# The PSUM banks of an MLP as tiles of their own, in a pool opened behind the first batch's attention

## The chip, the cores and the metric

The kernel runs on one core of a Trainium2 chip. The core has five engines with instruction queues of their own: TensorE (PE, the matmuls; PEld is its loading of weights), VectorE (DVE), ScalarE (ACT), GpSimd (POOL) and SyncE (SP), which here only issues DMA transfers. Matmuls write to PSUM, a memory of eight banks of 2 KB in each of 128 partitions; VectorE and ScalarE carry results from there to SBUF ("evacuate" them). The metric is the device time of one execution in microseconds (us); lower is better.

## What is computed

Four batches of causal-window attention with eight heads (sequence 768, head dimension 64), and then a Fourier mix with a two-layer MLP over its output:

```
scores = q @ k.T / 8 + bias                    # kept: 96 local keys, 8 global keys
a = exp(scores - max) / sum
x = (a @ v), heads side by side                # (4, 768, 512)
u = x + real(fft over the sequence and over the 512 columns)
un = (u - mean(u)) / sqrt(var(u) + 1e-6)
out = u + max(un @ w_ch1, 0) @ w_ch2           # w_ch1: 512 x 2048, w_ch2: 2048 x 512
```

## The kernel before

The work of a batch goes through these steps. `trans` turns q and k of two heads (L392, transposes on TensorE into a PSUM tile `pt`); `score` multiplies them (L420, into `sc`), ScalarE takes the exponential (`er`, L439), VectorE multiplies by the mask (`ex`, L449); `v_global` and `glob` treat the eight global keys; `av` multiplies with v (L519, L532, into `pav`) and VectorE divides (`rc` L549, `x` L550). The Fourier mix follows: folds on VectorE (`eA`, `ww`, `zy`, L592 to L661), matmuls `py` (L683, L686), mirrored copies on GpSimd, matmuls `pu` (L763), the sum `u` (L780), statistics (L789, L791) and `rstd` on GpSimd, the normalised `un` (L809, L811) and its transposes `ptu` (L827) into `unT` (L835, L837).

The MLP then runs in 12 groups `c` of 256 rows, three to a batch. The first layer is `ph_unit(c, jp)`, eight units to a group: eight matmuls of 128x256 (L855) into one bank `ph`, and one evacuation with the ReLU into `hT`, on ScalarE (L861) or VectorE (L862). The second layer is `pg_unit(c, t, part)`: for each of the two output tiles `t`, four parts of four matmuls of 128x512 (L878) that add up in one bank `pg`; then VectorE adds `u` (`ob`, L889) and SyncE stores it (L893).

The order of all instructions is fixed while the program is written: a planner (`Plan`) keeps an estimated time for each engine and picks from four streams (Fourier mix, attention, first layer, second layer) the step that can start first by its own table of costs. For the MLP it counts two free banks for `ph` and two for `pg` (`RING`). It also decides which of ScalarE and VectorE evacuates. Each engine then works through its instructions in order; the framework under the kernel puts in the waits, from which tiles an instruction reads and writes.

PSUM is split as follows. The tag `xx` has two tiles of two banks, used by all of attention and the Fourier mix. The other four banks are two tiles `c0` and `c1` of two banks each, allocated once and never given back (`cd`). While the first batch's attention runs, they are two more places for its scores and products (tags `C` and `D`). After that, a unit of the first layer writes one half of `c0`, in turn, and an output tile of the second layer one half of `c1`:

```
if tag in turn:
    turn[tag] += 1
    return cd["ph pg".index(tag) // 3][:, turn[tag] % 2, :]
```

A unit of the first layer may not be planned before all 22 uses of `C` and `D` in the first batch are through (the token `("CD",)`).

Of the kernel before, what the change touches and what calls it, by code (L numbers as in the profile page):

```python
# [10 lines left out]
FP32 = mybir.dt.float32  # L11
# [3 lines left out]
P = 128  # L15
# [156 lines left out]
def kernel(  # L172
# [69 lines left out]
    ps = ctx.enter_context(tc.tile_pool(name="ps", bufs=1, space=bass.MemoryType.PSUM))  # L242
# [3 lines left out]
    RING = {"xx": 2, "ph": 2, "pg": 2}  # L246
    pl.rings = {r: [0.0] * n for r, n in RING.items()}

    cd = [ps.tile([P, 2, 512], FP32, tag=f"c{i}", name=f"c{i}", bufs=1) for i in range(2)]
    pl.rings["C"] = [0.0]  # L250
    pl.rings["D"] = [0.0]
    turn = {"ph": 0, "pg": 0}

    def bank(tag, name, dtype=FP32):

        if tag in "CD":
            return cd["CD".index(tag)]
        if tag in turn:
            turn[tag] += 1
            return cd["ph pg".index(tag) // 3][:, turn[tag] % 2, :]  # L260
        return ps.tile([P, 2, 512 if dtype == FP32 else 1024], dtype, tag=tag, name=name, bufs=RING[tag])


    NBUF = {"hT": 3, "vs": 2, "qk": 2, "qs": 3, "qkT": 4, "er": 2, "eg": 1, "x": 1, "xr": 1, "zy": 1, "eA": 1,
# [118 lines left out]
    def trans(b, hp):  # L383
        n = HP * b + hp

        def run(start, ring):
            pt = bank("xx", f"pt_{n}", FP16)
            src = qk16.pop(n)
            for w in range(2):
                for j in range(NS):  # L390
                    o = pt[:, w, (j // 2) * 256:(j // 2) * 256 + 256].rearrange("p (a t m) -> p t a m", a=2, t=2)
                    nc.tensor.transpose(o[:, j % 2], src[:, w, j].rearrange("p h d -> p (h d)"), idn)  # L392
            e = pl.pe(mm_us(P, 2 * NS), start)
            pl.used(("free", "qk", n), e)

            def evac():
                TT[n] = buf("qkT", n, [P, 2, S], FP16, 6)
                V.tensor_copy(TT[n], pt[:, :, 0:S])  # L398
            pl.later([("DVE", dve2(2 * S), evac)], free("qkT", n), e, [("qkT", n)], ring=ring, rank=RA(b))
            for s in range(2):  # L400
                def cp(s=s):
                    c0 = 16 * (hp % 2) + 8 * s
                    nc.gpsimd.tensor_copy(  # L403
                        kG[b % 2][64 * s:64 * s + 64, hp, c0:c0 + NG].rearrange("p (j m) -> p j m", j=2),
                        TT[n][64 * s:64 * s + 64, 1, 0:P].rearrange("p (j m) -> p j m", j=2)[:, :, 0:NG // 2])
                pl.later([("POOL", 0.2, cp)], [("qkT", n)] + ([("gldone", b - 2, hp // 2)] if b > 1 else []), 0.0,
                         [("kG", n, s)], [("free", "qkT", n)], rank=RA(b))
        ATT.append(([("qk", n, 0), ("qk", n, 1)], ("xx",), run))

    def score(b, hp, g):  # L410
        n = HP * b + hp
        idx = 3 * n + g

        def run(start, ring):
            pa = bank(ring, f"sc_{n}_{g}")
            w0, w1_ = ((256, CO), (CO, CO), (256, P))[g]
            for i, c0, cw in ((2 * g, 0, w0), (2 * g + 1, 256, w1_)):
# [37 lines left out]
    def v_global(b, halves):  # L455
        def run(start, ring):
            pv = bank(ring, f"pvg_{b}_{halves[0]}")
            for half in halves:
                for h in range(4):
                    nc.tensor.matmul(pv[32 * half:32 * half + 32, 0, h * 64:(h + 1) * 64],  # L460
                                     sel_sb[:, h * 32:(h + 1) * 32],
                                     v16[b % 2][:, 0, 4 * half + h, 0:Dh], start=True, stop=True,
                                     tile_position=(0, 32 * half))
            e = pl.pe(mm_us(64, 4 * len(halves)), start)
            rows = slice(32 * halves[0], 32 * halves[-1] + 32)
            dst = vG[b % 2][rows, :, 0:Dh]
            src = pv[rows, 0, 0:256].rearrange("p (h d) -> p h d", d=Dh)
            pl.later([("ACT", act(256), lambda: A(dst, src, AF.Copy)),
                      ("DVE", dve(256), lambda: V.tensor_copy(dst, src))],
                     [("avdone", b - 2)] if b > 1 else [], e, [("vG", b, half) for half in halves], CD(b), ring=ring, rank=RA(b))  # L470
        ATT.append(([("v", b, 2 * half + i) for half in halves for i in range(2)] + [("one", 0)], BANKS(b), run))
# [581 lines left out]
```

## Time and profile before

| | us |
|---|---|
| median of 3 runs | 342.33 |
| lowest and highest | 341.27 to 342.86 |
| the profiled execution | 341.82 |
| its span, first to last instruction | 340.1 |
| TensorE busy | 269.9 |
| VectorE busy | 192.7 |
| ScalarE busy | 117.0 |
| GpSimd busy | 82.8 |

The span is the stretch that the profile shows; the execution's time holds 1.7 us more around it. Busy times count an engine's instructions as the profiler records them; matmuls are pipelined, and the record of the last one before a pause is longer than the time until the next one could have been issued. "c" in the rows stands for `c0` and `c1`, since buffer numbers are left out.

In order of time: up to 57 us the first batch's attention and its Fourier mix, with the loads of the weights; then three times a stage in which the first layer is mixed with the next batch's attention (from 57, 139 and 214 us) and one with that batch's Fourier mix and the second layer (from 106, 181 and 253 us); from 283 us the MLP alone, for what is left of it.

### The profile page before, as it was taken

How to read it: one execution, taken by the hardware profiler on the slowest of the kernel's cores; microseconds unless marked ns; L12 is line 12 of the kernel's file. 1: busy time of each engine (PE TensorE's matmuls, PEld its weight loads, DVE VectorE, ACT ScalarE, POOL GpSimd, SP SyncE). 2: the span in 40 equal slices, each digit the busy share in tenths (PEclk: the TensorE clock that was granted, in tenths of full speed). 3: DMA queues.
4: the chain of work that ended last, by engine and by line, in shares of the span. 5: the costliest groups of instructions: out<-in, count | busy, mean ns of one | idle time of the engine just before them, and what ended most of it. 6: DMA issues, size and time to landing. Idle time of an engine off the chain costs nothing.

```text
span 340.1 us, 5796 instructions
## 1 busy us (share of the span) xinstructions
PE 269.9 (79%) x2360; PEld 179.8 (53%) x2360; DVE 192.7 (57%) x348; ACT 117.0 (34%) x165; POOL 82.8 (24%) x165
## 2 busy tenths in 40 slices
PE   0687266888899796687889799977798998888984
PEld 0454154766665354566566356665574565666531
DVE  2579956553468968455368859655458487100011
ACT  7384022435640023345632132544621113323300
POOL 1351058335533505503005123300000053000000
PEclk9997565899999999599999999999999999999999
DMA  9999899999896950300205411000024301000011
GB/s 191 225 234 223 156 233 206 226 216 219 169 223 162 271 189 34 92 2 16 78 2 139 138 49 61 33 3 0 3 48 109 123 34 62 2 31 2 31 62 62
DMA packets 66091, 37.04 MB, mean 109 GB/s; under 512 B 26641, under 2 KB 61713, under 8 KB 66065
## 3 DMA queue, kind: packets, MB, share of 16 engines
q1 hardware_dynamic: 61840, 32.48, 39.9%
q0 software_dynamic: 4224, 4.19, 7.5%
q8 instruction: 18, 0.29, 0.4%
q14 instruction: 9, 0.07, 0.1%
HBM read 31.42 MB, written 9.44 MB: 120 GB/s over the span
## 4 chain that ended last, share of the span: by engine, by line
PE 59%; DVE 17%; ACT 10%; SPq 5%; issue 3%; POOL 3%; DMA 2%; DVEq 0%; POOLq 0%; ACTq 0%
PE c L855 27%; PE c L878 19%; ACT hT L861 8%; DVE hT L862 5%; DVE ob L889 3%; PE pav L532 3%; SPq L339 2%; DMA u<-in_v_dram 2%; PE py L683 2%; SPq L314 2%; PE pu L763 2%; PE py L686 1%; DVE x L550 1%; PE pav L519 1%; PE sc L420 1%
## 5 line engine op out<-in xcount | busy, mean ns | idle before, releaser
L855 PE MATMUL c<-unT,w 128*128 128x256 f16 x768 | 97.6, 278 | 25.4 <-ACT hT L861 17.4
L878 PE MATMUL c<-w,hT 128*128 128x512 f16 x384 | 91.4, 379 | 10.0 <-DVE ob L889 9.8
L855 PEld LDWEIGHTS <-w 128*128 128x128 f16 x768 | 75.1, 99 | 45.6 <-issue 34.5
L861 ACT ACTIVATE hT<-c 128x512 f16<-128x512 f32 x68 | 38.5, 595 | 86.9 <-PE c L855 68.5
L878 PEld LDWEIGHTS <-hT 128*128 128x128 f16 x384 | 36.7, 98 | 48.9 <-issue 13.9
L862 DVE TENSOR_SCALAR hT<-c 128x512 f16<-128x512 f32 x28 | 19.2, 691 | 49.5 <-PE c L855 48.4
L439 ACT ACTIVATE er<-sc 128x768 f16<-128x768 f32 (+2 forms) x42 | 38.3, 925 | 20.1 <-PE sc L420 9.9
L889 DVE TENSOR_TENSOR ob<-c,u 128x512 f32<-128x512 f32 x24 | 16.5, 689 | 45.9 <-PE c L878 45.9
L354 POOL CAST qk<-qs 128x768 f16<-128x768 f32 x24 | 23.1, 980 | 36.9 <-issue 34.5
L449 DVE TENSOR_TENSOR ex<-er,mk 128x992 f16<-128x992 f16 (+2 forms) x48 | 30.7, 657 | 0.4 <-ACT er L439 0.4
L699 ACT ACTIVATE zy<-py 128x512 f16<-128x512 f32 (+1 forms) x12 | 9.6, 810 | 58.9 <-PE py L686 47.9
L732 POOL COPY ww<-zy 128x512 f16<-128x512 f16 x16 | 9.4, 614 | 64.2 <-PE py L683 46.0
L403 POOL COPY kG<-qkT 64x8 f16<-64x8 f16 x32 | 9.9, 311 | 51.8 <-DVE qkT L398 51.0
L392 PE MATMUL pt<-ident,qk 128*128 128x128 f16 x192 | 16.5, 247 | 3.2 <-DVE qk L352 1.3
L683 PE MATMUL py<-t,ww 128*128 128x256 f16 x48 | 12.4, 308 | 7.8 <-DVE ww L646 6.9
L398 DVE COPY qkT<-pt 128x1536 f16<-128x1536 f16 x16 | 15.2, 952 | 5.5 <-PE pt L392 5.5
L809 ACT ACTIVATE un<-u,rstd 128x512 f16<-128x512 f32 x13 | 10.3, 808 | 22.2 <-POOL rstd L799 22.2
L392 PEld LDWEIGHTS <-qk 128*128 128x128 f16 x192 | 14.4, 112 | 5.7 <-issue 3.0
L420 PE MATMUL sc<-qkT 64*128 64x256 f16 (+2 forms) x168 | 15.2, 273 | 2.7 <-DVE u L780 2.1
L780 DVE TENSOR_TENSOR u<-pu,xr 128x1024 f32<-128x1024 f32 x12 | 14.4, 1219 | 4.6 <-PE pu L763 4.6
L532 PEld LDWEIGHTS <-ex 128*128 128x128 f16 x352 | 13.6, 100 | 5.7 <-issue 1.7
L532 PE MATMUL pav<-v,ex 128*128 128x65 f16 x308 | 15.3, 196 | 0.0
(89 smaller groups left out, 278.0 us busy)
## 6 DMA issues: line engine op xcount, KB each, us to landing
out_dram<-ob SPq DMA_DIRECT2D x24, 256.0 KB, 2.0
qs<-in_q_dram SPq DMA_DIRECT2D x13, 384.0 KB, 6.1
qs<-in_k_dram SPq DMA_DIRECT2D x13, 384.0 KB, 4.5
vs<-in_v_dram SPq DMA_DIRECT2D x24, 192.0 KB, 6.0
w<-in_moe_w_ch_dram POOLq DMA_DIRECT2D x8, 512.0 KB, 11.9
xd<-x SPq DMA_DIRECT2D x16, 192.0 KB, 3.6
xr<-xd SPq DMA_DIRECT2D x8, 384.0 KB, 3.8
u<-in_v_dram SPq DMA_DIRECT2D x8, 192.0 KB, 6.1
```

Of the source, the lines that this page charges most:

```text
L354: nc.gpsimd.tensor_copy(d, s)
L392: nc.tensor.transpose(o[:, j % 2], src[:, w, j].rearrange("p h d -> p (h d)"), idn)
L420: nc.tensor.matmul(pa[:, s, c0:c0 + cw], TT[n][lo:lo + 64, 1, i * P:(i + 1) * P], TT[n][lo:lo + 64, 0, i * P:i * P + cw], start=True, stop ...
L439: A(mine(), cut(pa), AF.Exp, 0.0, 0.125)
L449: VT(o, mine(), m, op=ALU.mult)
L532: nc.tensor.matmul(po[:, jj, hh * 65:(hh + 1) * 65], lhsT, v16[b % 2][:, i, h, 0:65], start=(jp == 0 and a == 0), stop=(a == len(ops) - 1) ...
L683: nc.tensor.matmul(o, wr, t1_sb[:, rs, 128:384], start=True, stop=(wi is None))
L855: nc.tensor.matmul(ph[:, a * CH:(a + 1) * CH], w1[:, d, jb * P:(jb + 1) * P], UNT[c][:, d, :], start=(d == 0), stop=(d == ND - 1))
L861: pl.later([("ACT", act(512), lambda: A(dst, ph, AF.Relu)), ("DVE", dve(512), lambda: V.tensor_scalar_max(dst, ph, 0.0))], [], e, [("h", c ...
L862: ("DVE", dve(512), lambda: V.tensor_scalar_max(dst, ph, 0.0))],
L878: nc.tensor.matmul(pg, HT[c][:, jb, t * P:(t + 1) * P], w2[:, jb, :], start=(jb == 0), stop=(jb == NJ - 1))
L889: VT(cell[0], pg, UT[c][:, t, :], op=ALU.add)
```

## The change

The four banks are no longer two tiles that stay. The early places `C` and `D` come from a pool of their own (`pse`), and each use allocates a tile anew. When the first bank for the MLP is asked for, that pool is closed and another (`psl`) is opened in its place, and from then on each unit of the first layer gets a tile of one bank under the tag `ph`, each output tile one under `pg`, with two buffers to a tag. The planner's numbers are untouched. Lines below the change are two higher than before (L855 becomes L857, L861 becomes L863, L878 becomes L880).

```diff
@@ -246,19 +246,21 @@
     RING = {"xx": 2, "ph": 2, "pg": 2}
     pl.rings = {r: [0.0] * n for r, n in RING.items()}
 
-    cd = [ps.tile([P, 2, 512], FP32, tag=f"c{i}", name=f"c{i}", bufs=1) for i in range(2)]
     pl.rings["C"] = [0.0]
     pl.rings["D"] = [0.0]
-    turn = {"ph": 0, "pg": 0}
+
+    early = {"ctx": tc.tile_pool(name="pse", bufs=1, space=bass.MemoryType.PSUM)}
+    early["pool"] = early["ctx"].__enter__()
 
     def bank(tag, name, dtype=FP32):
-
-        if tag in "CD":
-            return cd["CD".index(tag)]
-        if tag in turn:
-            turn[tag] += 1
-            return cd["ph pg".index(tag) // 3][:, turn[tag] % 2, :]
-        return ps.tile([P, 2, 512 if dtype == FP32 else 1024], dtype, tag=tag, name=name, bufs=RING[tag])
+        if tag in ("C", "D"):
+            return early["pool"].tile([P, 2, 512], FP32, tag=tag, name=name, bufs=1)
+        if tag == "xx":
+            return ps.tile([P, 2, 512 if dtype == FP32 else 1024], dtype, tag=tag, name=name, bufs=RING[tag])
+        if "late" not in early:
+            early["ctx"].__exit__(None, None, None)
+            early["late"] = ctx.enter_context(tc.tile_pool(name="psl", bufs=1, space=bass.MemoryType.PSUM))
+        return early["late"].tile([P, 512], FP32, tag=tag, name=name, bufs=RING[tag])
 
 
     NBUF = {"hT": 3, "vs": 2, "qk": 2, "qs": 3, "qkT": 4, "er": 2, "eg": 1, "x": 1, "xr": 1, "zy": 1, "eA": 1,
```

On every engine the instructions stand in the same order as before. What changes is what they wait for. On ScalarE, in the end phase (the eight units of group 10; `hT` is the ReLU's output, `c_66` is `c0`), before:

```order
L861 ACTIVATE hT_3415<-c_66 128x512
L861 ACTIVATE hT_3415<-c_66 128x512 [waits PE_49]
L861 ACTIVATE hT_3415<-c_66 128x512
L861 ACTIVATE hT_3415<-c_66 128x512 [waits PE_49]
L861 ACTIVATE hT_3415<-c_66 128x512
L861 ACTIVATE hT_3415<-c_66 128x512 [waits PE_49]
L861 ACTIVATE hT_3415<-c_66 128x512
L861 ACTIVATE hT_3415<-c_66 128x512 [waits PE_49]
```

and with the change:

```order
L863 ACTIVATE hT_3531<-ph_0_3532 128x512 [waits PE_49]
L863 ACTIVATE hT_3531<-ph_1_3549 128x512 [waits PE_49]
L863 ACTIVATE hT_3531<-ph_2_3558 128x512 [waits PE_49]
L863 ACTIVATE hT_3531<-ph_3_3573 128x512 [waits PE_49]
L863 ACTIVATE hT_3531<-ph_4_3582 128x512 [waits PE_49]
L863 ACTIVATE hT_3531<-ph_5_3597 128x512 [waits PE_49]
L863 ACTIVATE hT_3531<-ph_6_3608 128x512 [waits PE_49]
L863 ACTIVATE hT_3531<-ph_7_3625 128x512 [waits PE_49]
```

Before, every second evacuation waits for TensorE and the one behind it for nothing; now each one waits for TensorE, and each reads a tile of its own.

On TensorE, at the same place in the program (where the second unit of a pair follows the first, and then where the next pair follows a part of the second layer, whose output `c_67` is `c1`; `w` are the weights), before:

```order
L855 MATMUL c_66<-unT_3391,w_74 128x256
L855 LDWEIGHTS w_74
L855 MATMUL c_66<-unT_3391,w_74 128x256
L855 LDWEIGHTS w_74
L855 MATMUL c_66<-unT_3391,w_74 128x256
...
L878 MATMUL c_67<-w_75,hT_3290 128x512
L855 LDWEIGHTS w_74
L855 MATMUL c_66<-unT_3391,w_74 128x256 [waits Activation_49]
L855 LDWEIGHTS w_74
L855 MATMUL c_66<-unT_3391,w_74 128x256
```

and with the change:

```order
L857 MATMUL ph_1_3549<-unT_3504,w_75 128x256
L857 LDWEIGHTS w_75
L857 MATMUL ph_2_3558<-unT_3504,w_75 128x256 [waits Activation_49]
L857 LDWEIGHTS w_75
L857 MATMUL ph_2_3558<-unT_3504,w_75 128x256
...
L880 MATMUL pg_0_3516<-w_76,hT_3397 128x512
L857 LDWEIGHTS w_75
L857 MATMUL ph_3_3573<-unT_3504,w_75 128x256 [waits Activation_49]
L857 LDWEIGHTS w_75
L857 MATMUL ph_3_3573<-unT_3504,w_75 128x256
```

Before, only the first unit of a pair waits for ScalarE; now each unit waits for the evacuation of the unit that had its bank.

## Rows read from the trace of the kernel before

**Rows 1.** The page, part 1: busy us, share of the span, instructions.

```profile
PE 269.9 (79%) x2360; PEld 179.8 (53%) x2360; DVE 192.7 (57%) x348; ACT 117.0 (34%) x165; POOL 82.8 (24%) x165
```

**Rows 2.** The page, part 4: the chain that ended last, by line.

```profile
PE c L855 27%; PE c L878 19%; ACT hT L861 8%; DVE hT L862 5%; DVE ob L889 3%; PE pav L532 3%; SPq L339 2%; DMA u<-in_v_dram 2%; PE py L683 2%; SPq L314 2%; PE pu L763 2%; PE py L686 1%; DVE x L550 1%; PE pav L519 1%; PE sc L420 1%
```

**Rows 3.** The waits of TensorE: us in total, times, longest us.

```profile
PE c L855 <- ACT hT L861: 17.4, 30, 1.5
PE c L878 <- DVE ob L889: 9.8, 11, 1.8
...
PE c L855 <- DVE hT L862: 6.8, 11, 1.3
```

**Rows 4.** The timeline, TensorE, end phase: start, us, what [idle <-releaser].

```profile
300.89 1.91 PE L855 MATMUL c<-unT,w 128*128 128x256 f16 x16 [0.31 <-ACT hT L861]
302.63 1.03 PE L878 MATMUL c<-w,hT 128*128 128x512 f16 x4
303.97 1.91 PE L855 MATMUL c<-unT,w 128*128 128x256 f16 x16 [0.31 <-ACT hT L861]
```

**Rows 5.** The timeline, ScalarE, the same stretch.

```profile
302.83 1.09 ACT L861 ACTIVATE hT<-c 128x512 f16<-128x512 f32 x2 [1.99 <-PE c L855]
```

**Rows 6.** The timeline, all engines, the last output tiles.

```profile
329.04 3.61 PE L878 MATMUL c<-w,hT 128*128 128x512 f16 x16 [0.78 <-DVE ob L889]
```

**Rows 7.** The timeline, all engines, a stop with attention mixed in.

```profile
149.68 1.92 PE L855 MATMUL c<-unT,w 128*128 128x256 f16 x16
...
151.54 0.38 PE L420 MATMUL sc<-qkT 64*128 64x240 f16 x4
151.71 0.69 DVE L862 TENSOR_SCALAR hT<-c 128x512 f16<-128x512 f32 x1 [2.29 <-PE c L855]
...
152.44 0.60 ACT L861 ACTIVATE hT<-c 128x512 f16<-128x512 f32 x1 [1.59 <-DVE hT L862]
...
153.09 0.38 PE L855 MATMUL c<-unT,w 128*128 128x256 f16 x2 [1.17 <-ACT hT L861]
```

**Rows 8.** Tile c: count, ns min/median/max, first and last start.

```profile
L855 PE MATMUL c<-unT,w x768: 269/272/421, 57.3 to 320.1; 128*128 128x256 f16 x192
...
L861 ACT ACTIVATE hT<-c x68: 585/597/597, 59.2 to 320.4; 128x512 f16<-128x512 f32 x68
...
L862 DVE TENSOR_SCALAR hT<-c x28: 681/692/693, 62.9 to 287.8; 128x512 f16<-128x512 f32 x28
...
L550 DVE TENSOR_TENSOR x<-c,rc x3: 691/691/691, 21.2 to 32.4; 128x512 f16<-128x512 f32 x3
```

**Rows 9.** Groups of TensorE in 57.2:105.9, 139.4:180.9, 214.5:253.3, 283.4:340.1 (two rows).

```profile
L855 PE MATMUL c<-unT,w 128*128 128x256 f16 x192 | 24.8, 283 | 6.8 <-ACT hT L861 4.3 <-DVE hT L862 1.4 <-ACT unT L835 1.1
...
L855 PE MATMUL c<-unT,w 128*128 128x256 f16 x176 | 23.5, 285 | 7.5 <-ACT hT L861 5.9 <-DVE hT L862 1.6
...
L855 PE MATMUL c<-unT,w 128*128 128x256 f16 x169 | 21.4, 272 | 6.3 <-ACT hT L861 3.3 <-DVE hT L862 2.9
...
L855 PE MATMUL c<-unT,w 128*128 128x256 f16 x192 | 23.0, 272 | 4.4 <-ACT hT L861 3.5 <-DVE hT L862 0.9
...
L878 PE MATMUL c<-w,hT 128*128 128x512 f16 x101 | 24.2, 379 | 2.3 <-DVE ob L889 2.3
```

**Rows 10.** Stretches: us, busy of PE PEld DVE ACT POOL, clock, DMA share, GB/s.

```profile
57.20:105.90 48.70, 42.60 (x434) 31.28 (x434) 25.42 (x45) 21.50 (x32) 20.03 (x34) 0.96 1.08 206
180.90:214.50 33.60, 30.51 (x232) 17.50 (x230) 27.63 (x45) 8.53 (x11) 13.05 (x24) 1.00 0.27 87
```

**Rows 11.** The timeline, GpSimd, the first mixed stage.

```profile
71.92 0.83 POOL L365 CAST v<-vs 128x768 f16<-128x768 f32 x1 [1.14 <-DMA vs<-in_v_dram]
```

**Rows 12.** Stretches, three more, columns as in rows 10.

```profile
131.50:139.30 7.80, 3.79 (x49) 3.23 (x47) 7.19 (x16) 3.19 (x4) 2.94 (x8) 0.83 0.09 35
139.30:142.90 3.60, 3.54 (x18) 2.28 (x16) 0.00 (x0) 0.32 (x1) 2.96 (x6) 0.50 0.32 88
...
300.90:318.20 17.30, 15.75 (x117) 11.40 (x117) 1.38 (x2) 5.43 (x10) 0.00 (x0) 1.00 0.08 30
```

## The prediction

> **What bounds the kernel now.** I read the busy times first. TensorE works 79% of the span and VectorE 57% [rows 1]: TensorE is the fullest engine, so the question is why it stops. The chain that ended last answers: beside the matmuls of the MLP (27% and 19% of the span) the two evacuations `hT` (8% and 5%) and the output addition `ob` (3%) stand in it [rows 2]. A chain through an evacuation means that the matmuls stood still for it. The waits of TensorE give the sum: matmuls of the first MLP layer (L855) waited 17.4 us in 30 stops for ScalarE's evacuation and 6.8 us in 11 stops for VectorE's; the second layer (L878) waited 9.8 us in 11 stops for `ob` [rows 3]. That is 34.0 us in 52 stops.
>
> The timeline shows why. In the end phase TensorE runs 16 matmuls (two units of 8, one into each half of tile `c0`), then four of the second layer, and idles 0.31 us; then the same again, 3.08 us later [rows 4]. ScalarE starts at 302.83, which is 0.03 us after the end of the *second* unit (300.89 + 1.91 = 302.80), and evacuates both in one go of 1.09 us [rows 5]; TensorE restarts 0.05 us after that. The first unit's evacuation never runs beside the second unit's matmuls, though they touch different halves. The last output tiles show the same on `c1`: 16 matmuls start at 329.04, after 0.78 us of idling for `ob`, though `ob` reads the half that they don't write [rows 6]. So a tile of two banks is waited for as a whole, in both directions: a reader waits for every write before it, and a write for every reader.
>
> In the stages where attention is mixed in, it is worse: VectorE's evacuation at 151.71 waits for the second unit, ScalarE's at 152.44 waits for VectorE's (another half of the same tile), and TensorE restarts at 153.09 after 1.17 us [rows 7].
>
> **The change, part by part.** *Order.* No instruction moves on any engine; each evacuation gets a wait of its own, and each unit of the first layer too, as the order shows. So the sum is about waits alone.
>
> *A stop costs more than its idle time.* A pair's 16 matmuls are issued in 1.74 us (300.89 to 302.63), but the recorded run is 1.91 us: the last 0.17 us is a tail that the next matmul covers when it follows directly [rows 4]. Before a stop it is lost. Four matmuls of the second layer are issued in 0.86 us (1.03 recorded, less the same tail). So the work of a pair with its part is 2.60 us, and 3.08 - 2.60 = 0.48 us is lost, 0.31 of it idle. All stops: 34.0 + 52 x 0.17 = 42.8 us.
>
> *What the exact waits give back in the end phase.* The first unit ends at 300.89 + 0.87 + 0.17 = 301.93. ScalarE can start 0.03 later, takes 0.60 [rows 8], and 0.05 later the bank is free: 302.61, when TensorE has just issued the second unit (302.63) and has four more matmuls to do. The stop is gone. Where nothing stands between, the margin is 0.02 us for ScalarE; VectorE's 0.69 us evacuation comes 0.07 us late. 28 such evacuations [rows 8] make 2.0 us at most that stays. For `ob` the 16 matmuls of the next output tile last 3.61 us [rows 6], longer than the 0.78 us that it takes to the restart: hidden. The end phase has 4.4 us of idle on L855 [rows 9] and 2.3 on L878 [rows 9]; with the tails over 9 us comes back here.
>
> *In the mixed stages* (6.8, 7.5 and 6.3 us idle on L855, 1.1 of the first for `unT` [rows 9]) an evacuation can stand behind an exponential on ScalarE. Walk the stop of [rows 7]: the first unit of 149.68 ends by 150.72, VectorE evacuates it by 151.44 and not by 152.40; ScalarE takes the second at 151.6; the four score matmuls between keep TensorE until about 151.9, and then the bank is free. The 1.17 us vanish. Bounds for what stays there: nothing, as in this walk, or all of it (19.5 us idle), the second rival. I take 0.8 us, nearest the walk.
>
> *In the stages of the Fourier mix* the stops are on L878, 9.8 - 2.3 = 7.5 us [rows 3]: `ob` stands behind the folds on VectorE. With a second bank the next output tile goes on meanwhile. What comes next there is VectorE itself: 27.6 of 33.6 us busy in one such stretch [rows 10]; with a third of the 7.5 us and its tails gone, some 3 us, the stretch would still be longer than VectorE's work.
>
> *The pool that opens late.* The first `ph` may wait for the last readers of the early pairs. The last of them starts at 32.4, the first L855 at 57.3 [rows 8]: 25 us of cover, so nothing. If the cover were gone the price would be one `x` of 0.69 us. The stage up to 57 us is unchanged.
>
> *Loads.* Faster matmuls ask earlier for the second batch's data, while the DMA engines are full until 106 us (share 1.08 [rows 10]). The last cast of that stage that waited for a transfer is at 71.92, after 1.14 us [rows 11]. The cost lies between nothing and all that this stage could gain, 5.7 us idle [rows 9] and its tails; I take nothing, since the casts after it waited for none.
>
> **Sum.** 42.8 - 2.0 - 0.8 = 40.0 us. The profiled execution took 341.8 us (span 340.1), so 301.8; the median of the runs shown lies 0.5 us above it. Forecast: 302 us.
>
> **A rule against it.** The rows say that TensorE stands still for evacuations and restarts 0.05 us behind them [rows 3 to 5]. The Trainium skill, *TensorE: Matmul & The Clock Gate*, section "HAM oscillation — how this bites in real kernels", tells of a matmul kernel in which double buffering of PSUM gave no further gain; by that this would stay at 342 us. Here the waits name the evacuations themselves, so the sum goes by the rows, and the rule is left a chance below.
>
> **The rivals.**
> *Half of it is kept.* In the mixed stages ScalarE and VectorE do their exponentials and products in a fixed order, and the stop only changes its name: the unit waits for an evacuation that stands behind `er`. For it: 41 of the stops release from engines that serve attention too, and the margin is 0.02 us. Against it: the walk. Then only the end phase and the Fourier stages gain, 6.7 + 7.5 = 14.2 of 34.0 us idle, or 42% of 42.8: 18 us, 324 us. With half of the other 58% (12.4 us) back as well, and 2.0 us off, it is 313.
> *The loads bound batch 1.* The first mixed stage then gains nothing: 5.7 of the 34.0 us idle, so 7.2 of the 42.8: 309 us. For it the share of 1.08; against it that casts hardly wait after 72 us.
> *The clock falls, and it is slower.* At 139.3 to 142.9 the granted clock is 0.50 (1.2 GHz) after a stretch in which TensorE was busy 3.79 of 7.80 us [rows 12], half the level of the end phase. If denser stretches broke into short pauses that let the clock go, each of the 48 pairs (768 matmuls of L855 by 16) would take twice its 1.74 us; with 25 of them at the low level the gain of 42.8 us is eaten. Against it: the end phase, with a pause every 3.08 us, is granted 1.00 (2.4 GHz) [rows 12], and the pauses get fewer. The skill's same page, section "A second HAM failure mode: psum-queue depth-cycling", describes such a loss in a kernel that cycled through PSUM banks; no run here shows it.
> *Nothing comes of it:* either the waits stay coarse after all, or TensorE stands as long for the next thing in each place; 342 us. Against the first speak the order's separate waits, against the second the walk, in which nothing else is late. The second is what the skill's rule above comes to.
>
> **How the numbers follow.** Forecast case (296 to 308 us) 0.73; loads 0.06; half kept (310 to 325) 0.13; slower 0.03; no change 0.03 (0.02 for coarse waits, 0.01 for the skill's rule); more than 46 us gained 0.02. More could come only from the idle times that are not these stops, which I leave untouched. The range 295 to 314 takes in the first case, the loads and the milder half of the second rival, about 0.83. Half a per cent, 1.7 us, is what a measurement of this kernel can tell from no change. Faster by more: 0.73 + 0.06 + 0.13 + 0.02 = 0.94; within: 0.03; slower: 0.03.
>
> **What would show it.** Right: in the waits, L855 behind `hT` under 6 us in all and L878 behind `ob` under 1; single evacuations of 0.60 us in the end phase in place of runs of two, and 2.60 us from pair to pair; the chain with over 70% TensorE and `hT` under 5%; TensorE's busy time down by about 9 us (the tails), to 261. Half kept: many L855 stops whose releaser `hT` began late behind `er`. Loads: casts waiting for transfers at 60 to 80 us. Clock: granted 0.50 in the end phase. The forecast is wrong if L855 waits over 10 us in all, or if as many microseconds show up as new waits of `py`, `pu` or `ptu`.

## The result, and the profile after

The changed kernel takes **300.28 us** (median of 4 runs, 298.73 to 302.98); the kernel before took 341.88 us beside it (4 runs, 341.27 to 342.86). The ratio is 0.8789, 95% interval 0.8721 to 0.8857: faster by 41.6 us, where 302.0 us had been forecast. Two more comparisons gave 301.11 us (ratio 0.8773, 0.8701 to 0.8845) and 302.21 us (0.8828, 0.8789 to 0.8867). In each of these two, one execution fell into a slower state; the medians hold it, the ratios leave it out. The profiled execution is the slowest of the first four, 302.98 us with a span of 301.2; the one before had a span of 340.1. So the two traces differ by 38.9 us of the 41.6, and the account below is of these 38.9; the other 2.7 lie between executions.

The busy times, as in [rows 1]:

```profile
PE 264.0 (88%) x2360; PEld 178.5 (59%) x2360; DVE 193.8 (64%) x348; ACT 119.0 (40%) x165; POOL 85.0 (28%) x165
```

The number of matmuls is the same, and TensorE's idle time is 301.2 - 264.0 = 37.2 us where it was 340.1 - 269.9 = 70.2: 33.0 us of idling are gone. The other 5.9 us of the 38.9 are TensorE's busy time, 269.9 to 264.0. Where the idling went, the waits of TensorE tell (us in total, times, longest; the first seven rows of eighteen, and three further down):

```profile
PE pones L938 <- DMA ident<-idm: 7.5, 1, 7.5
PE py L685 <- DVE ww L648: 6.5, 1, 6.5
PE pvg L462 <- POOL v L367: 2.7, 2, 1.4
PE pu L765 <- POOL rev L722: 2.2, 1, 2.2
PE sc L422 <- DVE u L782: 2.1, 2, 1.3
PE ptu L829 <- ACT un L811: 1.6, 1, 1.6
PE py L685 <- DVE qkT L400: 1.5, 1, 1.5
...
PE sc L422 <- DVE qkT L400: 1.2, 2, 1.1
PE ph L857 <- ACT unT L837: 1.1, 1, 1.1
PE pt L394 <- ACT unT L837: 1.1, 1, 1.1
```

The three rows of [rows 3], 34.0 us in 52 stops, have no successor: no matmul of `ph` or `pg` waits for `hT` or `ob` at all. The one wait that `ph` still has is for its input `unT`, as before. The groups of the page say the same, the last column being the idle time before them:

```profile
L857 PE MATMUL ph<-unT,w 128*128 128x256 f16 x768 | 97.9, 279 | 1.1 <-ACT unT L837 1.1
L880 PE MATMUL pg<-w,hT 128*128 128x512 f16 x384 | 89.8, 379 | 0.0
L863 ACT ACTIVATE hT<-ph 128x512 f16<-128x512 f32 x68 | 40.6, 597 | 55.3 <-PE ph L857 54.1
L864 DVE TENSOR_SCALAR hT<-ph 128x512 f16<-128x512 f32 x28 | 19.4, 692 | 25.2 <-PE ph L857 25.0
```

One direction is left: the evacuations wait for the matmuls (54.1 and 25.0 us), as they did before (68.5 and 48.4 us for matmuls), but no matmul waits for them. A reading lesson lies in the first row: the sum of L857's durations is 97.9 us, no less than before (97.6), though TensorE's busy time fell. Each recorded run holds its own tail; where the next run follows directly, the tail lies under that run, and the engine's busy time counts the overlap once.

The chain that ended last, by engine:

```profile
PE 70%; DVE 12%; SPq 6%; POOL 3%; ACT 3%; DMA 2%; issue 2%; POOLq 0%; ACTq 0%
```

ScalarE's `hT` had 8% of it alone [rows 2], and now the whole engine has 3%.

The end phase on TensorE, against [rows 4]:

```profile
267.69 1.91 PE L857 MATMUL ph<-unT,w 128*128 128x256 f16 x16
269.44 1.03 PE L880 MATMUL pg<-w,hT 128*128 128x512 f16 x4
270.30 1.91 PE L857 MATMUL ph<-unT,w 128*128 128x256 f16 x16
```

From pair to pair 2.61 us (270.30 - 267.69) instead of 3.08, and no idle time. ScalarE in the same stretch, against [rows 5]:

```profile
268.76 0.60 ACT L863 ACTIVATE hT<-ph 128x512 f16<-128x512 f32 x1 [1.14 <-PE ph L857]
269.64 0.60 ACT L863 ACTIVATE hT<-ph 128x512 f16<-128x512 f32 x1 [0.28 <-PE ph L857]
```

Two evacuations of their own take the place of one run of two; the first begins at 268.76, while the second unit's matmuls still run (to 267.69 + 1.91 = 269.60), as the walk in the prediction had it. The output tiles at the end have no stop either: one run of 60 matmuls.

```profile
284.23 13.11 PE L880 MATMUL pg<-w,hT 128*128 128x512 f16 x60
```

By stretches (columns as in rows 10, us; busy of PE, PEld, DVE, ACT, POOL; clock; DMA share; GB/s), most of the first mixed stage and 140 to 290 us:

```profile
57.20:97.00 39.80, 39.50 (x394) 29.01 (x394) 24.42 (x41) 22.29 (x32) 20.11 (x34) 0.92 1.11 206
...
140.00:290.00 150.00, 149.81 (x1341) 101.26 (x1340) 92.91 (x162) 62.09 (x88) 25.27 (x55) 1.00 0.18 56
```

and 140 to 290 us of the kernel before:

```profile
140.00:290.00 150.00, 129.60 (x1172) 86.21 (x1171) 94.34 (x165) 52.17 (x72) 28.11 (x62) 0.99 0.19 56
```

TensorE is busy 149.81 of 150 us, where it was busy 129.60. There is nothing left to take from waits between 140 and 290 us: the kernel is bound there by TensorE at a granted clock of 1.00 (2.4 GHz).

### The profile page after: what moved, and what is told of

Its sections match the earlier page's. It is cut to its first block, busy times and chain, and to the rows that moved or that the text cites. A ratio compares the mean times of both kernels' runs of the same rounds, so it can differ in the third digit from the quotient of the medians.

```text
span 301.2 us, 5772 instructions
## 1 busy us (share of the span) xinstructions
PE 264.0 (88%) x2360; PEld 178.5 (59%) x2360; DVE 193.8 (64%) x348; ACT 119.0 (40%) x165; POOL 85.0 (28%) x165
## 4 chain that ended last, share of the span: by engine, by line
PE 70%; DVE 12%; SPq 6%; POOL 3%; ACT 3%; DMA 2%; issue 2%; POOLq 0%; ACTq 0%
PE ph L857 29%; PE pg L880 21%; PE pav L534 4%; PE sc L422 3%; SPq L341 3%; SPq L316 3%; DMA u<-in_v_dram 2%; PE py L685 2%; PE pt L394 2%; PE ptu L829 2%; PE pu L765 2%; PE pav L521 2%; PE py L688 2%; ACT er L441 1%; DVE ob L891 1%
## 5 line engine op out<-in xcount | busy, mean ns | idle before, releaser
L857 PE MATMUL ph<-unT,w 128*128 128x256 f16 x768 | 97.9, 279 | 1.1 <-ACT unT L837 1.1
L880 PE MATMUL pg<-w,hT 128*128 128x512 f16 x384 | 89.8, 379 | 0.0
L857 PEld LDWEIGHTS <-w 128*128 128x128 f16 x768 | 73.3, 100 | 18.3 <-issue 6.1
L863 ACT ACTIVATE hT<-ph 128x512 f16<-128x512 f32 x68 | 40.6, 597 | 55.3 <-PE ph L857 54.1
L880 PEld LDWEIGHTS <-hT 128*128 128x128 f16 x384 | 36.7, 98 | 36.8 <-issue 0.8
L441 ACT ACTIVATE er<-sc 128x992 f16<-128x992 f32 (+2 forms) x48 | 43.4, 922 | 21.0 <-PE sc L422 18.8
L891 DVE TENSOR_TENSOR ob<-pg,u 128x512 f32<-128x512 f32 x24 | 16.5, 688 | 32.5 <-PE pg L880 31.9
L864 DVE TENSOR_SCALAR hT<-ph 128x512 f16<-128x512 f32 x28 | 19.4, 692 | 25.2 <-PE ph L857 25.0
L356 POOL CAST qk<-qs 128x768 f16<-128x768 f32 x24 | 24.2, 1020 | 30.5 <-issue 23.0
L701 ACT ACTIVATE zy<-py 128x512 f16<-128x512 f32 (+1 forms) x12 | 9.6, 810 | 54.1 <-PE py L688 50.1
L422 PE MATMUL sc<-qkT 64*128 64x256 f16 (+1 forms) x192 | 16.9, 279 | 3.3 <-DVE u L782 2.1
L534 PE MATMUL pav<-v,ex 128*128 128x65 f16 x352 | 18.3, 200 | 0.7 <-DVE ex L451 0.6
```

The costliest lines, as they stand in the source:

```text
L356: nc.gpsimd.tensor_copy(d, s)
L422: nc.tensor.matmul(pa[:, s, c0:c0 + cw], TT[n][lo:lo + 64, 1, i * P:(i + 1) * P], TT[n][lo:lo + 64, 0, i * P:i * P + cw], start=True, stop ...
L441: A(mine(), cut(pa), AF.Exp, 0.0, 0.125)
L534: nc.tensor.matmul(po[:, jj, hh * 65:(hh + 1) * 65], lhsT, v16[b % 2][:, i, h, 0:65], start=(jp == 0 and a == 0), stop=(a == len(ops) - 1) ...
L857: nc.tensor.matmul(ph[:, a * CH:(a + 1) * CH], w1[:, d, jb * P:(jb + 1) * P], UNT[c][:, d, :], start=(d == 0), stop=(d == ND - 1))
L863: pl.later([("ACT", act(512), lambda: A(dst, ph, AF.Relu)), ("DVE", dve(512), lambda: V.tensor_scalar_max(dst, ph, 0.0))], [], e, [("h", c ...
```

## The experiments

All start from the changed kernel. First it was taken apart: which of its two halves (exact waits for `ph`, exact waits for `pg`) gives what, and does the late pool itself give or cost anything.

**The changed kernel again**, on the chip of the next three.

> The changed kernel once more, beside the runs that follow: 300 us, as measured before (298.7 to 303.0). It is what each part alone is held against.

Measured: 301.11 us (299.11 to 304.28), the kernel before 342.54 us on this chip (13 runs). By the ratio, 0.8773, the gain to share out here is 42.0 us (39.6 to 44.5).

**Exact waits for `ph` alone.** The two `pg` banks become the halves of one tile again:

```diff
@@ bank(), ahead of its last return
+        if tag in ("pg",):
+            if tag not in early:
+                early[tag] = early["late"].tile([P, 2, 512], FP32, tag=tag, name=tag + "w", bufs=1)
+                early[tag + "n"] = 0
+            early[tag + "n"] += 1
+            return early[tag][:, early[tag + "n"] % 2, :]
```

> The first layer's two banks are tiles of their own, the second layer's two stay one tile that is waited for as a whole. Theory (each stop costs its idle time and a tail of 0.17 us, and the two layers' stops are independent): the 41 stops of the first layer go, 17.4 + 6.8 + 41 x 0.17 = 31.2 us, so 341.9 - 31.2 = 311 us, and the second layer's waits behind ob stay near 9.8 us in 11 stops. Rival (the stops are coupled: a unit that is no longer held is held at the next part of the second layer): over 320 us, with far more than 9.8 us behind ob.

Measured: 311.83 us (310.73 to 312.48), ratio 0.9102 (0.9047 to 0.9158): 30.7 us gained, about 11 missing. The waits of TensorE begin with

```profile
PE pgw L886 <- DVE ob L897: 9.3, 11, 1.6
```

and hold none of `ph` for `hT`. The 11 stops for `ob` are back, 9.3 us where they were 9.8, and no stop for `hT`.

**Exact waits for `pg` alone.** The same edit for `"ph"` in place of `"pg"`.

> The other half: the second layer's two banks are tiles of their own, the first layer's two stay one tile. Theory: the 11 stops behind ob go, 9.8 + 11 x 0.17 = 11.7 us, so 330 us; the first layer's waits stay near 24.2 us in 41 stops. Rival (the layers are coupled): 336 us or more, the time coming back as longer first-layer waits. The gains of this run and the one before add up to the 42 us of the whole change by the theory, to clearly less or more by the rival.

Measured: 330.80 us (330.45 to 331.46), ratio 0.9662 (0.9606 to 0.9718): 11.7 us gained. Its waits of TensorE:

```profile
PE phw L863 <- ACT hT L869: 17.2, 29, 1.5
...
PE phw L863 <- DVE hT L870: 6.8, 11, 1.2
```

The two halves make 30.7 + 11.7 = 42.4 us against 42.0 together: within the intervals they add up, so neither kind of stop hides behind the other. And they give the price of a stop by itself. The 41 stops for `hT` idled 24.2 us [rows 3] and were worth 30.7: 6.5 / 41 = 0.16 us for each beyond its idle time (0.11 to 0.21 by the interval of the ratio). The 11 for `ob` idled 9.8 and were worth 11.7: 1.9 / 11 = 0.17, though the interval of its ratio, 1.9 us either way, can't tell this second figure from nothing.

**The late pool with whole tiles.** The same edit for both tags: the pool opens late, the early pairs are tiles of their own, but `ph` and `pg` are halves again.

> The early places come from a pool of their own and the MLP's banks from one opened late, as in the change, but the MLP's four banks are two tiles of two banks again, used by halves. Theory (only the size of the tile counts): 342 us, within 2 us of the kernel before, with 24 us behind the evacuations and 10 us behind ob. Rival (the fresh tiles of the early places or the late pool bring part of it): 338 us or less.

Measured: 341.36 us (340.66 to 343.18, 10 runs), ratio 0.9970 (0.9940 to 0.9999). Its waits of TensorE are [rows 3] again:

```profile
PE phw L863 <- ACT hT L869: 17.4, 30, 1.5
PE pgw L886 <- DVE ob L897: 9.8, 11, 1.8
PE phw L863 <- DVE hT L870: 6.8, 11, 1.2
```

So the gain is in the tiles of one bank, and not in the pool, which is worth 2 us at most by the interval. TensorE's busy time gives a second, rougher figure for what a stop costs beyond its idle time: 270.5 us here, 264.3 with `ph` exact, 268.6 with `pg` exact, so 6.2 / 41 = 0.15 and 1.9 / 11 = 0.17 us for each stop; from the halves on to the whole change (264.0) it is 4.6 / 41 = 0.11 and 0.3 / 11 = 0.03. Three traces of the changed kernel have 263.9, 264.0 and 265.3 us, so a microsecond there tells little.

**One pool from the start.** What is the late opening there for? Here `ph` and `pg` have their four single banks from the beginning, and batch 0's attention has `xx` alone in place of `xx`, `C` and `D` (an excerpt: the making of the early pool and the waits for the token `("CD",)` go too):

```diff
-        if "late" not in early:
-            early["ctx"].__exit__(None, None, None)
-            early["late"] = ctx.enter_context(tc.tile_pool(name="psl", bufs=1, space=bass.MemoryType.PSUM))
-        return early["late"].tile([P, 512], FP32, tag=tag, name=name, bufs=RING[tag])
+        return ps.tile([P, 512], FP32, tag=tag, name=name, bufs=RING[tag])
@@ BANKS(b)
-        return ("xx", "C", "D") if b == 0 else ("xx",)
+        return ("xx",)
@@ CD(b)
-        return [("CD",)] if b == 0 else []
+        return []
```

> No early places at all: the first batch's attention uses the two xx tiles alone, and the MLP's four banks are tiles of one bank each from the one pool that is open from the start. Theory (the size of the tile counts, not when its pool opens): no wait of the first or second layer behind its evacuations, as in the changed kernel; the first batch loses two places for its scores, which costs 0 to 6 us (six exponentials of 0.97 us read them), so 300 to 307 us. Rival (the late pool matters by itself): waits behind hT and ob come back, 5 us or more of them.

Measured: 304.17 us (302.10 to 305.21), ratio 0.8909 (0.8873 to 0.8944) to the kernel before beside it (341.04 us, 11 runs). Tile `ph` and two stretches (columns as above):

```profile
L848 PE MATMUL ph<-unT,w x768: 271/273/421, 65.4 to 282.0; 128*128 128x256 f16 x192
```

```profile
25.00:57.00 32.00, 19.70 (x163) 12.59 (x161) 23.45 (x53) 7.73 (x11) 6.29 (x13) 0.98 0.89 182
57.00:66.00 9.00, 5.92 (x52) 4.89 (x51) 7.11 (x13) 3.68 (x5) 7.46 (x17) 0.69 1.21 194
```

No stop behind `hT` or `ob` here either, so most of the gain needs no late pool. Its ratio lies above the changed kernel's three by 0.008 to 0.014, and its interval just above theirs (0.8873 against 0.8867 at the nearest), so the early pairs are worth about 1% (the changed kernel did not run beside it). They are worth less than the first MLP matmul suggests, which comes 7.9 us later here (65.4 against 57.5): in this kernel TensorE was granted 0.98 at 25 to 57 us, the changed one 0.67 in the same stretch, and the mean over the span is 0.983 against 0.943.

**After the stops: VectorE in batch 1's Fourier mix.** The new wait of the changed kernel, `py` for `qkT`, is 1.5 us here and 0.9 in two more traces of the same kernel. It lies behind VectorE in a Fourier stage, as the prediction had it, though in batch 1's and not in batch 2's [rows 10]. TensorE there, and VectorE:

```profile
101.97 12.25 PE L880 MATMUL pg<-w,hT 128*128 128x512 f16 x56
115.77 0.28 PE L685 MATMUL py<-t,ww 128*128 128x256 f16 x1 [1.55 <-DVE qkT L400]
```

```profile
106.11 1.04 DVE L606 TENSOR_TENSOR zy<-eA,ww 128x512 f16<-128x512 f16 x1
...
114.76 0.95 DVE L400 COPY qkT<-pt 128x1536 f16<-128x1536 f16 x1
```

From 100.22 to 115.71 VectorE works without a gap, and the copy at its end frees the PSUM pair that `py` takes. So that copy was allowed to run on ScalarE (an excerpt: `evac` gets the engine as an argument):

```diff
-            pl.later([("DVE", dve2(2 * S), evac)], free("qkT", n), e, [("qkT", n)], ring=ring, rank=RA(b))
+            pl.later([("DVE", dve2(2 * S), lambda: evac("DVE")), ("ACT", act(2 * S), lambda: evac("ACT"))][:2 if b else 1],
+                     free("qkT", n), e, [("qkT", n)], ring=ring, rank=RA(b))
```

> From the changed kernel: the copy of the transposed q and k out of PSUM may go to ScalarE as well as to VectorE in batches 1 to 3, whichever the planner finds earlier (five of twelve go there). Theory (after the change VectorE's folds are the next thing late: py waited 1.5 us for such a copy that stood behind them): that wait goes, and with VectorE relieved of 5 x 0.95 us the time falls by 1.5 to 3 us, to 297.5 to 299. Rival (TensorE is nearly full after 57 us, and the copies were covered): 300 to 301, or the same wait behind ScalarE.

Measured: 301.63 us (300.68 to 303.84, 6 runs), ratio 0.8844 (0.8811 to 0.8878): no gain over the changed kernel, whose ratios are 0.8773 to 0.8828. My theory missed. The wait of `py` for `qkT` is gone, but ScalarE needs 1.45 us for the copy that takes VectorE 0.95, and stops come up elsewhere:

```profile
PE ptu L832 <- ACT qkT L401: 2.2, 1, 2.2
...
PE sc L425 <- ACT er L444: 1.1, 1, 1.1
```

**VectorE without GpSimd beside it.** In the rows above L606 took 1.04 us; in batch 3 the same instruction takes 0.42. GpSimd casts `q`, `k` and `v` of the next batch beside the folds of batches 1 and 2, and nothing beside those of batch 3. So the casts of `q` and `k` went to ScalarE; those of `v` stayed, and beside L606 it was mostly one of these (105.86 to 106.88):

```diff
-            ways = [("POOL", 0.9, lambda: cast("POOL"))]
+            ways = [("ACT", act(768), lambda: cast("ACT"))]
```

> All 24 casts of q and k of batches 1 to 3 move from GpSimd to ScalarE (GpSimd keeps the casts of v). Theory: VectorE's folds of batches 1 and 2 took about twice as long as those of batch 3 because GpSimd's casts ran beside them (L600 1.20 us against 0.69 of the same shape, L606 1.04 against 0.42); without them the folds of batches 1 and 2 take what batch 3's take (sum of the 128x1536 and 128x1024 fold instructions down by some 3 us in each batch), and VectorE's busy time falls by 4 to 8 us. The time: 295 to 299 us if VectorE's chain in the Fourier stage of batch 1 is what holds that stage. Rival A: the folds keep their durations, the casts are not the cause. Rival B: the folds get shorter, but the time stays at 300 to 303 us, since TensorE is busy nearly all of 140 to 290 us and ScalarE's 20 us more of casts come ahead of exponentials and evacuations.

The changed kernel ran once more beside it.

> The changed kernel again, for the comparison on the same chip: 299 to 302 us.

Measured: 303.75 us (301.59 to 304.42, 6 runs), ratio 0.8884 (0.8852 to 0.8915), and the changed kernel 302.21 us (299.13 to 304.20). Groups of VectorE, line, operation, shapes, count, busy us and mean ns, in the changed kernel of this comparison:

```profile
L595 DVE TENSOR_TENSOR eA<-x 128x1536 f16<-128x1536 f16 x3 | 4.1, 1366 | 0.0
L600 DVE TENSOR_TENSOR ww<-eA 128x1024 f16<-128x1024 f16 x3 | 3.1, 1026 | 0.1
L601 DVE TENSOR_TENSOR ww<-eA 128x1024 f16<-128x1024 f16 x3 | 3.3, 1098 | 0.0
```

and with the casts on ScalarE:

```profile
L595 DVE TENSOR_TENSOR eA<-x 128x1536 f16<-128x1536 f16 x3 | 2.9, 951 | 0.0
L600 DVE TENSOR_TENSOR ww<-eA 128x1024 f16<-128x1024 f16 x3 | 2.1, 692 | 0.1
L601 DVE TENSOR_TENSOR ww<-eA 128x1024 f16<-128x1024 f16 x3 | 2.1, 685 | 0.0
```

About the folds the theory held: rival A falls, and VectorE's busy time is down from 193.4 to 188.2 us, though the big folds (L594, L595, L600, L601) gave 1.9 us in each of the two batches where 3 had been expected. About the time rival B held: nothing is gained, since TensorE was busy 150.00 of the 150 us from 140 to 290, and before that stretch the wait of `py` for `qkT` gave way to longer ones for ScalarE (`ptu` for `un` 3.7 us in 3 instead of 1.5 in 1, and 2.0 us of `pu` for `er`). No version was found that beats the changed kernel.

## Why the prediction was right

**What bounds it, and the whole-tile waits: right, and shown.** The stops were read as waits for a tile of two banks, in both directions. With the late pool but tiles of two banks, all 52 are there; with single banks, none.

**34.0 us idle: right. 52 x 0.17 us of tails: right in kind, too much in size.** The idle time of TensorE fell by 33.0 us, 34.0 of stops less 1.0 by which the rest of its idle time grew. The tail of 0.17 us was read from one row of the end phase [rows 4] and used for all stops, but it depends on what stands ahead of the stop. Two rows of the changed kernel, where nothing waits any more:

```profile
75.80 0.59 PE L422 MATMUL sc<-qkT 64*128 64x256 f16 x8
76.33 1.92 PE L857 MATMUL ph<-unT,w 128*128 128x256 f16 x16
```

The next unit starts 0.06 us ahead of the recorded end of the score matmuls (75.80 + 0.59 - 76.33). In the trace of before, 19 of the 52 stops stand behind a score matmul or one of `pvg`, with 0.07 us each, and 33 behind matmuls of the second layer, transpositions and others, with 0.16: 19 x 0.07 + 33 x 0.16 = 6.6 us, where the sum had 8.8. The times of the halves (0.11 to 0.21 for a stop of `ph`) are too coarse to settle this; the rows are what shows it, and the profile models the ends of matmuls in them.

**2.0 us that stay for VectorE's evacuations, and 0.8 us in the mixed stages: both too much; measured 0.** The 2.0 us were a bound ("at most") that the sum took as the value. The 0.07 us of lateness counts only where a third unit follows two directly. The recorded runs of `ph` are 34 of one unit, 29 of two and one of four: behind every second unit stands something else, but for the one run of four, whose first two units ran mostly at half the clock (0.50 at 130.0 to 132.9 us, 0.80 on to 138.0) and so took longer. A stage with attention mixed in shows how it goes; TensorE, VectorE and ScalarE, 198 to 202 us:

```profile
198.01 1.91 PE L857 MATMUL ph<-unT,w 128*128 128x256 f16 x16
199.75 1.03 PE L880 MATMUL pg<-w,hT 128*128 128x512 f16 x4
200.62 0.61 PE L829 MATMUL ptu<-ident,un 128*128 128x128 f16 x8
201.06 1.04 PE L857 MATMUL ph<-unT,w 128*128 128x256 f16 x8
```

```profile
199.08 0.69 DVE L864 TENSOR_SCALAR hT<-ph 128x512 f16<-128x512 f32 x1 [0.18 <-PE ph L857]
```

```profile
199.96 0.60 ACT L863 ACTIVATE hT<-ph 128x512 f16<-128x512 f32 x1 [0.42 <-PE ph L857]
```

VectorE takes the first unit while the second still runs, ScalarE the second 0.04 us after its end (198.01 + 1.91 = 199.92); both are through by 200.56, and the next unit begins at 201.06. The evacuations of one pair no longer stand behind each other.

**The Fourier stages: right in kind.** VectorE was named as what is late next, and the new 1.5 us wait of `py` is that. With 1.5 us it is more than the 1.0 us by which the other idle time grew in all; smaller ones shrank. In batches 2 and 3 no such wait came up.

**TensorE's busy time: forecast down by about 9 us, measured 5.9.** The tails of 6.6 us instead of 8.8 (above) are 2.2 of the 2.9 missing. The rest lies where TensorE worked longer at the lower clock. A row of the changed kernel:

```profile
60.42 3.29 PE L857 MATMUL ph<-unT,w 128*128 128x256 f16 x16
```

The same matmuls took 2.55 us in the kernel before: 0.7 us. From the last stretch at the low clock on (135 us; 144 before) both kernels were granted 1.00. There the busy time fell by 5.5 us over 39 stops, or 0.14 each (11 x 0.07 + 28 x 0.16 = 5.3 by the tails), the same in all three traces of the changed kernel. So the number came out by luck in part: 2.9 us too much for the busy time and 2.8 us that did not stay cancel, with the 1.0 us of other idle time on top: 40.0 forecast for the difference of the profiled executions, 38.9 measured. The median's 300.28 against 302 has a second accident in it: the forecast put the median 0.5 us above the profiled execution, as before, and here it lies 2.7 us below.

**No price for the late pool and the loads: right, the second narrowly.** The stage up to the first `ph` is unchanged (57.48 us against 57.28). The first mixed stage, from the first `ph` to the last `x` of batch 1, lasts 42.7 us (57.48 to 100.22) and lasted 48.6: 5.9 us came back, so the loads did not hold it. But they are close. In the kernel before, no cast of that stage waited for a transfer after 71.92 us [rows 11]; now most of them do, and the one at the first folds for 4.78 us:

```profile
101.88 1.57 POOL L367 CAST v<-vs 128x768 f16<-128x768 f32 x1 [4.78 <-DMA vs<-in_v_dram]
```

TensorE is busy 39.50 of 39.80 us in that stretch, so here it did not wait for them. In the trace of the changed kernel beside the next runs (304.28 us) it did: 1.9 us for GpSimd's `kG` and 0.8 for a cast of `qk`, both in a row of casts that had waited for transfers.

**The rivals.** *Half of it kept* falls by the waits: none is left behind `hT`, in the mixed stages either. *The clock falls* falls by the granted clock of 1.00 from 140 to 290 us; the time lost at the low clock over the whole span hardly grew either, (1 - 0.950) x 340.1 = 17.0 us before and (1 - 0.943) x 301.2 = 17.2 after. *Nothing comes of it* falls by the time; the rule of the Trainium skill that stood beside it ("TensorE: Matmul & The Clock Gate", "HAM oscillation — how this bites in real kernels": no further gain from PSUM double buffering in the kernel told of there) is not what these runs show. Here the kernel with the late pool and whole tiles and the one with single banks differ by 40 us (341.36 and 301.11).

## What to carry to other kernels

Two halves of one PSUM tile are no double buffer where waits are kept per tile: look for a reader that starts 0.03 us after the *last* write to the tile and runs over both halves in one go, and give each bank a tile of its own. Price such a stop as its idle time plus the tail of the matmul ahead of it, read for each kind of matmul (here 0.16 us behind the second layer and 0.07 behind scores), and look at what stands between two uses of the same bank before you keep a remainder for lateness. Where TensorE was busy nearly all of a stretch, relief for VectorE in or ahead of it gave nothing in either of two tries, even where it worked as meant.

## What was not expected of the hardware

**VectorE beside GpSimd.** A VectorE addition of two fp16 tensors took up to two and a half times as long while GpSimd casts: L606 1.04 us at 106.11 against 0.42 in batch 3 (and 0.41 in the trace of the last comparison, where no cast fell beside it), the 128x1024 folds 1.03 and 1.10 us on average against 0.69 with the casts moved away. GpSimd pays too: its casts of `q` and `k` took 0.81 us at the least and up to 1.56, and the cast of `v` at 101.88 took 1.57 beside a fold (L595, 101.82) that kept its 0.95. The Trainium skill, *SBUF — State Buffer*, section "Who interferes with whom", says that a VectorE instruction with two SBUF inputs contends with a GpSimd instruction that reads SBUF; the rows agree.

**The clock in a fuller early stage.** With fewer PSUM tiles for batch 0's attention the granted clock at 25 to 57 us was 0.98 instead of 0.67, and TensorE was busy 19.70 of the 32 us instead of 17.23. The MLP began 7.9 us later there, but the kernel ended only 2 to 4 us later; how much of the difference the clock made up, no run here tells. Three traces of the changed kernel were granted 0.67, 0.64 and 0.50 there, and the one at 0.50 has the shortest span (299.9 us). Nor is a higher mean clock a shorter time: of 24 executions of the kernel before, beside the first six experiments, the six granted 0.975 or 0.98 over the span took 342.85 to 345.28 us, the 18 granted 0.939 to 0.955 took 340.18 to 342.77.
